# First 64 positions of a retention layer: loads of eight positions a partition, 64x64 score quadrants, keys turned back with the decay

## The chip, the core and the metric

The kernel runs on one core of a Trainium2 chip. The metric is the device time of one execution in microseconds; the number given for a kernel is the median of several executions. TensorE (PE) does the matrix products and writes to PSUM; VectorE (DVE), ScalarE (ACT) and GpSimd (POOL) do the elementwise work; SyncE (SP) only issues transfers. ACT and POOL issue transfers as well, POOL also those that change the type from float32 to float16 on the way.

## What is computed

A retention layer (attention without softmax, with a decay by distance), then a two-layer network with a hard-swish between its layers. Eight batches, eight heads, 576 positions, 64 columns a head; 4608 tokens of 512 columns, 2048 hidden columns.

```python
def _attn_ref(q, k, v):                       # q, k, v: (8, 8, 576, 64)
    scores = D_ ** -0.5 * np.matmul(q, k.transpose(0, 1, 3, 2))
    gamma = 1.0 - 2.0 ** (-5.0 - np.arange(H))
    rel = pos[:, None] - pos[None, :]
    Dmat = np.where(rel >= 0, gamma[:, None, None] ** rel[None, :, :], 0.0)
    return np.matmul(scores * Dmat[None, :, :, :], v)

def _moe_ref(x, w_in, w_out):                 # x: (4608, 512), heads side by side
    h = x @ w_in
    g = h * np.clip(h + 3.0, 0.0, 6.0) / 6.0
    return g @ w_out
```

## The kernel before

**Blocks.** The 576 positions of a batch are cut into the first 64 (`TL`) and four chunks of 128. Block 0 of the network holds the first 64 positions of all eight batches (512 tokens); blocks 1 to 8 hold the 512 other positions of a batch each. Retention runs chunk by chunk with a state of 64x64 a head that is carried along (`zh` from the first 64 positions, then `z`). The network multiplies a block by `w_in` in 16 units (`up_steps`, `ph` products, four steps of 128 rows of `w_in` each), applies the hard-swish on ACT and DVE (L535, L537) and multiplies by `w_out` (`down_plain`, `pd` products; from block 2 on in a seven-product scheme, `pm`).

**Order.** The order of every engine's instructions is the order of the program text; nothing is rearranged. An engine that waits holds up all that stands behind it in its queue. From L771 to L831 the text is the work on the first positions, and the change lies in it, in the functions that it calls, and in `head_states`.

**First positions, loads (L407).** Head pair i holds heads 2i and 2i+1. `load_half` brings one head of q or k of all batches: partition r*8 + b holds positions 4r to 4r+3 of batch b, a row of 256 numbers (1 KB). The source pattern is `r b (j d)` with r of 16. Keys of pair 0 are issued on SP and ACT, queries of pair 0 and 1 on both, queries of pairs 2 and 3 on SP behind the landing of the first half of the keys (`keys`), keys of pairs 1 to 3 on POOL in float16 (2 and 3 behind `keys`). Then POOL issues all values in one transfer (`load_values`, `raw_v`), the first quarter of `w_in` in two halves (rows 0 to 255, then 256 to 511 of `w_in`, L683), and a further quarter. What POOL computes stands behind these issues.

**First positions, work.** `cast_heads` (DVE) turns float32 into float16. `turn_heads` (L440) is eight products against the permuted identity `by_chunk`; each gives one transposed piece of 64x128, columns in the order chunk, batch half, r; ACT copies them out of PSUM (`hqT`, `hkT`). A chunk c of this order is two batches, 128 tokens. `scores_heads` (L471) multiplies 128 keys by 128 queries of a chunk, both batches at once, so half of each result belongs to two different batches. The mask `hmask` (128 columns a head, by ACT from the distances in `dist`) carries the decay and is zero there and above the diagonal; DVE multiplies (`ha`). `values_heads` brings the values into the order of the keys by 16 products of 128x32 a pair (`by_key`), ACT copies. `inner_heads` (L485) multiplies values by masked scores, and one copy a pair puts the result into `xT0`, the input of the network. A few products without use (`idle_products`) stand between.

**First positions, states.** POOL multiplies the float16 keys by a decay for each position (`others`, L138). `keys_heads` (L466) brings a pair into the order of the keys by 16 products, and ACT writes it twice with a factor of 0 or 1 for each partition (`only`), so that `kn[0]` holds the first batch of a chunk and `kn[1]` the second, with zeros elsewhere. `head_states` (L290) makes both states from them. These run at L844, between `pd` products of block 0: `k0 D4 k1 D4 +1 k2 D4 +1 k3 D6 h0 D2 ...` stands for keys of pair 0, four steps of `down_plain`, and so on; `+1` is a pending DVE subtraction on the weights (L552), `h` a call of `head_states`.

Of the kernel before, what the change touches and what calls it, by code (L numbers as in the profile page):

```python
# [21 lines left out]
def kernel(  # L22
# [9 lines left out]
    nc = tc.nc  # L32
# [34 lines left out]
    RP = TL // NJ  # L67
    ii = const.tile([P, NJ + 1], I32)
    ij = const.tile([P, NJ + 6], I32)
    fj = const.tile([P, NJ + 6], FP32)  # L70
    key, odd = fj[:, NJ + 3:NJ + 4], fj[:, NJ + 5:NJ + 6]
    arg = const.tile([P, NJ + 3, 2 * H], FP32)
    dec = const.tile([P, NJ + 3, 2 * H], FP32)
# [5 lines left out]
    query = const.tile([P, P], FP32)  # L79
    early = io.tile([P, H, D], FP32, tag="fv", name="early").rearrange("p h d -> p (h d)")  # L80
    dist, far = early[:, 0:P], early[:, P:2 * P]
    scale = const.tile([P, 1], FP32)
    FAR = 1.0e6
    by_chunk = const.tile([P, P], FP16)
    only = const.tile([P, 2], FP32)
    last = const.tile([P, 1], FP32)
# [3 lines left out]
    def indices():  # L90
        nc.vector.memset(half, 0.5)
        nc.gpsimd.iota(ii[:, 0:NJ], pattern=[[0, NJ]], base=0, channel_multiplier=1)
        nc.gpsimd.iota(ii[:, NJ:NJ + 1], pattern=[[1, 1]], base=0, channel_multiplier=1)
        nc.gpsimd.iota(query, pattern=[[TL, 2], [1, NJ], [NJ, RP]], base=0, channel_multiplier=0,
                       allow_small_or_imprecise_dtypes=True)
        make_identity(nc, ident16)
        p_ = ii[:, NJ:NJ + 1]
        nc.vector.tensor_scalar(ij[:, 0:NJ], ii[:, 0:NJ], P - B, 1, ALU.bitwise_and, ALU.logical_shift_right)
        nc.vector.tensor_copy(ij[:, NJ:NJ + 1], p_)
        for e in range(2):  # L100
            nc.vector.tensor_scalar(ij[:, NJ + 1 + e:NJ + 2 + e], p_, SUB - 1, 1, ALU.bitwise_and,
                                    ALU.logical_shift_left)
        nc.vector.tensor_scalar(ij[:, NJ + 3:NJ + 4], p_, RP - 1, 2, ALU.bitwise_and, ALU.logical_shift_left)
        nc.vector.tensor_scalar(ij[:, NJ + 4:NJ + 5], p_, 5, None, ALU.logical_shift_right)
        nc.vector.tensor_scalar(ij[:, NJ + 5:NJ + 6], p_, 4, 1, ALU.logical_shift_right, ALU.bitwise_and)
        nc.vector.tensor_copy(fj, ij)
        nc.vector.tensor_tensor(fj[:, 0:NJ], fj[:, 0:NJ], query[:, 0:TL:RP], ALU.add)
        nc.vector.tensor_scalar(fj[:, NJ:NJ + 2], fj[:, NJ:NJ + 2], 1.0, -float(P // 2), ALU.mult, ALU.add)
        nc.vector.tensor_scalar(fj[:, NJ + 2:NJ + 3], fj[:, NJ + 2:NJ + 3], 1.0, 1.0 - float(P // 2), ALU.mult, ALU.add)
        nc.vector.tensor_copy(by_chunk.rearrange("p (c e r) -> p c e r", c=NCB, e=2),  # L110
                              ident16.rearrange("p (r e c) -> p c e r", e=2, c=NCB))

    def distances():
        nc.vector.memset(scale, float(np.log(D ** -0.5)))
        nc.vector.tensor_tensor(key, key, fj[:, NJ + 4:NJ + 5], ALU.add)
        nc.vector.scalar_tensor_tensor(out=key, in0=odd, scalar=float(TL), in1=key, op0=ALU.mult, op1=ALU.add)
        nc.vector.tensor_scalar(last, odd, float(TL), float(TL) - 0.5, ALU.mult, ALU.add)
        nc.vector.tensor_scalar(dist, query, key, FAR, ALU.is_lt, ALU.mult)
# [4 lines left out]
    def mask_of_heads(i):  # L123

        for h in (2 * i, 2 * i + 1):
            nc.scalar.activation(hmask[:, h, :], dist, ACTF.Exp, bias=scale, scale=float(np.log(gamma[h])))
# [791 lines left out]
```

## Time and profile before

| | us |
|---|---|
| median of 3 runs | 299.28 (299.08 to 300.13) |
| the profiled execution | 299.44 |
| its span, first to last instruction | 297.7 |
| mean granted TensorE clock, share of full speed | 0.994 |

The page of a profile gives each engine's busy time, the span in 40 slices, the DMA queues with packets and bytes, the chain of work that ended last (followed back from the last instruction to what released each step), and the costliest groups of instructions by line and shape. Further views give the instructions in order of time, the transfers with the time from issue to landing, and the busy time in chosen stretches. `L168` is line 168 of the kernel; the product helper is there, so groups are told apart by names such as `ph` or `pd`. PEld is the loading of weights into TensorE. Landing times of the first transfers, from the DMA view (issue and time to landing):

| transfer | issued on | issue | to landing |
|---|---|---|---|
| hk, pair 0, first and second half | SP, ACT | 0.82, 0.82 | 3.1, 2.6 |
| hk, pairs 1 to 3, six halves | POOL | 1.84 to 5.7 | median 4.8 |
| hq, eight halves | SP, ACT | 1.51 to 5.8 | 4.3 to 5.2 |
| raw_v, 512 KB in float16 | POOL | 6.17 | 7.9 |
| win, first half | POOL | 7.04 | 8.3 |
| win, last piece | POOL | 9.9 | 15.2 |
| wout, last piece | POOL | 15.60 | 19.8 |

Of the engines in the first 20 us, by stretches of 4 us:

| stretch | PE busy | DVE | ACT | POOL | clock |
|---|---|---|---|---|---|
| 0 to 4 | 2.05 | 2.72 | 1.49 | 2.39 | 1.00 |
| 4 to 8 | 2.71 | 1.86 | 2.67 | 3.84 | 1.00 |
| 8 to 12 | 3.52 | 2.67 | 3.58 | 3.81 | 1.00 |
| 12 to 16 | 1.86 | 2.95 | 1.92 | 0.93 | 0.97 |
| 16 to 20 | 4.00 | 0.94 | 1.79 | 3.49 | 0.60 |

### The profile page before, as it was taken

How to read it: one execution, taken by the hardware profiler on the slowest of the kernel's cores; microseconds unless marked ns; L12 is line 12 of the kernel's file. 1: busy time of each engine (PE TensorE's matmuls, PEld its weight loads, DVE VectorE, ACT ScalarE, POOL GpSimd, SP SyncE). 2: the span in 40 equal slices, each digit the busy share in tenths (PEclk: the TensorE clock that was granted, in tenths of full speed). 3: DMA queues.
4: the chain of work that ended last, by engine and by line, in shares of the span. 5: the costliest groups of instructions: out<-in, count | busy, mean ns of one | idle time of the engine just before them, and what ended most of it. 6: DMA issues, size and time to landing. Idle time of an engine off the chain costs nothing.

```text
span 297.7 us, 12581 instructions
## 1 busy us (share of the span) xinstructions
PE 286.3 (96%) x5552; PEld 218.8 (73%) x5552; DVE 211.3 (71%) x374; ACT 193.8 (65%) x350; POOL 133.4 (45%) x169
## 2 busy tenths in 40 slices
PE   5699999999999999999999999999999999999995
PEld 2467566788556667878988787787787788778894
DVE  5629636669885688798866887787769676647654
ACT  5659875789776687586758577566856665655420
POOL 7665078417851912539614862386256013100510
PEclk9979999999999999999999999999999999999999
DMA  7999998989999999998999999789907101200114
GB/s 163 188 205 216 217 233 206 213 184 221 135 214 221 203 205 196 167 234 191 228 244 194 184 216 174 144 168 263 144 27 118 74 2 39 104 5 2 73 73 141
DMA packets 119430, 47.86 MB, mean 161 GB/s; under 512 B 92240, under 2 KB 114768, under 8 KB 119376
## 3 DMA queue, kind: packets, MB, share of 16 engines
q1 hardware_dynamic: 114336, 41.56, 70.6%
q0 software_dynamic: 4608, 5.11, 10.4%
q8 instruction: 43, 0.70, 1.0%
q10 hardware_dynamic: 432, 0.39, 0.5%
q14 instruction: 11, 0.09, 0.2%
HBM read 36.70 MB, written 9.44 MB: 155 GB/s over the span
## 4 chain that ended last, share of the span: by engine, by line
PE 87%; DVE 4%; DMA 4%; ACT 3%; issue 1%; POOL 1%; ACTq 0%
PE ph L168 41%; PE pm L168 29%; PE pd L168 7%; PE po L250 4%; DMA raw_v<-in_v_dram 3%; PE pa L250 2%; DVE ws L552 2%; PE pu L250 1%; DMA hk<-in_k_dram 1%; ACT u L515 1%; DVE g L516 1%; DVE a L285 1%; POOL hk L416 1%; PE hpo L491 1%; PE hpv L459 1%
## 5 line engine op out<-in xcount | busy, mean ns | idle before, releaser
L168 PE MATMUL ph<-xT,win 128*64 128x512 f16 (+1 forms) x1248 | 144.9, 365 | 0.5 <-DVE g L516 0.3
L537 DVE SCALAR_TENSOR_TENSOR g<-u,ph 128x512 f16<-128x512 f32 x132 | 89.2, 683 | 48.5 <-ACT u L535 47.7
L535 ACT ACTIVATE u<-ph,half 128x512 f32<-128x512 f32 x132 | 90.2, 693 | 43.1 <-PE ph L168 40.6
L168 PEld LDWEIGHTS <-win 128*64 128x64 f16 x1248 | 84.5, 136 | 26.5 <-issue 1.9
L168 PEld LDWEIGHTS <-g 128*64 128x64 f16 x928 | 51.0, 110 | 15.6 <-issue 1.1
L168 PEld LDWEIGHTS <-s 128*64 128x64 f16 x896 | 49.9, 110 | 8.4 <-issue 0.5
L334 POOL TENSOR_TENSOR z<-z,gpow 128x256 f32<-128x256 f32 x24 | 16.4, 685 | 75.3 <-DVE z L333 46.9
L168 PE MATMUL pm<-ws,s 128*64 128x256 f16 x672 | 45.6, 273 | 0.1
L386 ACT CAST xT<-po 128x256 f16<-128x256 f32 (+1 forms) x44 | 22.5, 584 | 23.4 <-PE po L250 23.4
L211 POOL TENSOR_TENSOR q<-fq,dec 128x512 f16<-128x512 f32 x32 | 36.7, 1169 | 0.0
L214 POOL TENSOR_TENSOR v<-fv,dec 128x512 f16<-128x512 f32 x32 | 35.5, 1113 | 1.9 <-DMA fv<-in_v_dram 1.9
L168 PE MATMUL pd<-wout,g 128*64 128x512 f16 x256 | 35.0, 382 | 0.2 <-ACT o L581 0.2
L616 POOL TENSOR_TENSOR u<-u,p 128x512 f32<-128x512 f32 x7 | 8.9, 1271 | 54.0 <-ACT u L656 47.8
L168 PE MATMUL pm<-wout,g 128*64 128x256 f16 x448 | 31.6, 273 | 0.4 <-issue 0.4
L285 DVE TENSOR_TENSOR a<-pa,mask 128x256 f16<-128x256 f32 (+1 forms) x44 | 21.9, 539 | 7.8 <-PE pa L250 7.4
L203 ACT CAST k<-fk 128x512 f16<-128x512 f32 x32 | 19.8, 620 | 0.0
L552 DVE TENSOR_TENSOR s<-g 128x1024 f16<-128x1024 f16 x28 | 19.6, 702 | 0.2
L340 ACT CAST z<-z 128x512 f16<-128x512 f32 x24 | 15.0, 625 | 4.2 <-DVE z L330 3.9
L168 PE MATMUL pm<-ws,g 128*64 128x256 f16 x224 | 16.3, 273 | 0.0
L168 PE MATMUL pm<-wout,s 128*64 128x256 f16 x224 | 16.0, 273 | 0.1
L250 PE MATMUL po<-qT,z 64*64 64x64 f16 x512 | 12.6, 198 | 0.7 <-issue 0.4
L552 DVE TENSOR_TENSOR s<-g,s 128x1024 f16<-128x1024 f16 x14 | 12.6, 903 | 0.0
(112 smaller groups left out, 277.7 us busy)
## 6 DMA issues: line engine op xcount, KB each, us to landing
fq<-in_q_dram SPq DMA_DIRECT2D x16, 512.0 KB, 5.9
fk<-in_k_dram SPq DMA_DIRECT2D x32, 256.0 KB, 4.6
fv<-in_v_dram SPq DMA_DIRECT2D x32, 256.0 KB, 5.7
out_dram<-o SPq DMA_DIRECT2D x14, 512.0 KB, 3.2
wout<-in_moe_w_out_dram POOLq DMA_DIRECT2D x4, 512.0 KB, 18.5
out_dram<-o SPq DMA_DIRECT2D x7, 256.0 KB, 3.9
win<-in_moe_w_in_dram POOLq DMA_DIRECT2D x3, 512.0 KB, 13.4
hq<-in_q_dram SPq DMA_DIRECT2D x6, 128.0 KB, 5.0
```

What stands on the lines that cost most here:

```text
L168: nc.tensor.matmul(out[r], lhs[:, r], rhs, skip_group_check=True, **flags)
L203: keys = lambda: nc.scalar.copy(by_head(k16), in_rows(st[c]["fk"]))
L211: nc.gpsimd.tensor_tensor(by_head(q16[:, e]), in_rows(st[c]["fq"][:, :, e, :]), in_rows(dd[:, NJ + 1 + e, 0:H, :]), ALU.mult)
L214: nc.gpsimd.tensor_tensor(v16, st[c]["fv"], dd[:, NJ, H:2 * H, :], ALU.mult)
L250: return lambda: nc.tensor.matmul(*args, skip_group_check=True, **flags)
L285: nc.vector.tensor_tensor(a16[:, a, 0:n].rearrange("p x i q -> p (x i) q"), pa[a].rearrange("p x i q -> p (x i) q"), m, ALU.mult)
L334: nc.gpsimd.tensor_tensor(new, new, decay, ALU.mult)
L340: nc.scalar.copy(z16, zs[c])
L386: nc.scalar.copy(xt[:, s], po[s].rearrange("p x n (e r) -> p x n e r", e=2))
L535: nc.scalar.activation(uu, ph, ACTF.Relu, bias=half, scale=1.0 / 6.0)
L537: nc.vector.scalar_tensor_tensor(out=g[:, hf, :, jr, :], in0=by_half(uu), scalar=1.0, in1=by_half(ph), op0=ALU.min, op1=ALU.mult)
L552: nc.vector.tensor_tensor(*pend.popleft())
```

## The change

Pairs are now heads i and i+4, and group g holds pairs 2g and 2g+1. A transfer brings a whole pair: partition r*16 + (batch, head of the pair) holds positions 8r to 8r+7, a row of 512 numbers (2 KB); r counts 8. The keys are ordered by batch halves: partitions 0 to 63 take batch c, 64 to 127 batch c+4, so that chunk c is batches c and c+4. `turn_heads` has 16 products of 64 columns. The scores are 64x64 quadrants, a batch each, with masks of 64 columns; four products of DVE over two pairs replace eight. `values_heads` has 32 products for two neighbouring heads, against a selection (`selv`) that has zeros for the other half of the positions. `inner_heads` handles a group; ACT and DVE copy one half each. The keys for the states are the turned keys, turned back by eight products and multiplied by the decay on DVE; the copies on ACT, the factors `only` and POOL's products with the decay are gone, and the states read one half of the partitions each. The halves of the first quarter of `w_in` are now rows 0-127 and 256-383, then the others, and block units take the steps in the order 0, 2, 1, 3.

```diff
-    def load_half(i, nm, e, queue, behind=None):
...
-        d = queue.dma_start(hd[i][nm][:, e].rearrange("p j d -> p (j d)"),
-                            dict(q=q, k=k, v=v)[nm][:, 2 * i + e, 0:TL, :].rearrange("b (r j) d -> r b (j d)", j=NJ))
+    def load_heads(i, nm, queue, behind=None):
...
+        d = queue.dma_start(t, dict(q=q, k=k)[nm][:, i::NP, 0:TL, :].rearrange("b e (r j) d -> r (b e) (j d)", j=JL))
...
     def turn_heads(i, nm, copy):
...
-                nc.tensor.matmul(pt[e * D:e * D + D, j, :], hd[i][nm][:, e, j, :], by_chunk, start=True, stop=True,
+                nc.tensor.matmul(pt[e * D:e * D + D, at, :], hd[i][nm][:, j * D:j * D + D], sel[:, e], start=True, stop=True,
...
+    def values_heads(cc, copy):
+
+        pv = psum.tile([P, NCB, 2, D], FP32, tag="pp", name=f"hpv{cc}")
         for c in range(NCB):
+            for x in range(2):
+                for b2 in range(2):
+                    for jp in range(2):
+                        o = slice(SUB * b2 + SUB // 2 * jp, SUB * b2 + SUB // 2 * jp + SUB // 2)
+                        nc.tensor.matmul(pv[o, c], selv[:, x, NCB * b2 + c].rearrange("p y j r -> p (y j r)"),
+                                         raw_v[0][:, 2 * cc:2 * cc + 2, 2 * jp + x, :],
+                                         start=(c == 0 and x == 0), stop=(x == 1), skip_group_check=True)
+        copy(vh[:, :, cc], pv)
...
     def keys_heads(i):
-        pk = by_key(i, "k").rearrange("p c e d -> p c (e d)")
-        for e in range(2):
-            nc.scalar.mul(kn[e][:, i], pk, only[:, e:e + 1])
+        kT = hd[i]["kT"]
+        pk = psum.tile([P, NCB, 2, D], FP32, tag="pp", name=f"hpk{i}")
+        for c in range(NCB):
+            for b2 in range(2):
+                nc.tensor.matmul(pk[rows(b2), c], kT[:, NCB * b2 + c, :], ident16.rearrange("p (e d) -> p e d", e=2),
+                                 start=True, stop=True, skip_group_check=True)
+        dd = dec[:, 0, H + i::NP].unsqueeze(1).unsqueeze(3).to_broadcast([P, NCB, 2, D])
+        nc.vector.tensor_tensor(kn[:, i].rearrange("p c (e d) -> p c e d", e=2), pk, dd, ALU.mult)
+
+    def scores_heads(g):
+        a16 = work.tile([P, 2, 2, NCB, TL], FP16, tag="a16", bufs=4, name=f"ha16_{g}")
+        pa = [psum.tile([P, 2, NCB, TL], FP32, tag="pp", name=f"hpa{e}_{g}") for e in range(2)]
+        for x in range(2):
+            kT, qT = hd[2 * g + x]["kT"], hd[2 * g + x]["qT"]
+            for c in range(NCB):
+                for b2 in range(2):
+                    for e in range(2):
+                        b = NCB * b2 + c
+                        nc.tensor.matmul(pa[e][rows(b2), x, c, :], kT[rows(e), b, :], qT[rows(e), b, :],
+                                         start=True, stop=True, skip_group_check=True)
         for e in range(2):
+            m = hmask[:, NP * e + 2 * g:NP * e + 2 * g + 2, :].unsqueeze(2).to_broadcast([P, 2, NCB, TL])
+            nc.vector.tensor_tensor(a16[:, e], pa[e], m, ALU.mult)
...
+    def inner_heads(g):
...
+        po = [psum.tile([P, 2, NCB, TL], FP32, tag="pp", name=f"hpo{b2}_{g}") for b2 in range(2)]
+        for e in range(2):
+            for c in range(NCB):
+                for x in range(2):
+                    for b2 in range(2):
+                        nc.tensor.matmul(po[b2][rows(x), e, c, :], vh[rows(b2), c, 2 * e + g, x, :], a16[rows(b2), e, x, c, :],
+                                         start=True, stop=True, skip_group_check=True)
+        xt = xts[0][:, g::2, :].rearrange("p e (c b q) -> p b e c q", c=NCB, b=2)
+        nc.scalar.copy(xt[:, 0], po[0])
+        nc.vector.tensor_copy(xt[:, 1], po[1])
```

In `head_states` the left factor becomes `kn[rows(e), i, c, a * D:a * D + D]` and the right one `vh[rows(e), c, j, h2, :]`, with a PSUM bank for each of the two states. The order of the text:

```diff
-        for nm in ("k", "q"):
-            landed = load_half(0, nm, 0, sp)
-            keys = landed if nm == "k" else keys
-            load_half(0, nm, 1, act)
+        keys = load_heads(0, "k", sp)
+        load_heads(0, "q", act)
         nc.scalar.activation(warm, half, ACTF.Exp)
-        load_half(1, "q", 0, sp)
-        load_half(1, "q", 1, act)
+        load_heads(1, "q", sp)
         for i in (2, 3):
-            for e in range(2):
-                load_half(i, "q", e, sp, keys)
+            load_heads(i, "q", sp, keys)
         for i in (1, 2, 3):
-            for e in range(2):
-                load_half(i, "k", e, pool, None if i == 1 else keys)
+            load_heads(i, "k", pool, None if i == 1 else keys)
         load_values()
...
         idle_products(5)
-        mask_of_heads(0)
+        masks_of(0)
         cast_heads(0, "k", on_dve)
         turn_heads(0, "k", on_act)
-        mask_of_heads(1)
-        idle_products(4)
         cast_heads(0, "q", on_dve)
-        mask_of_heads(2)
+        idle_products(2)
         turn_heads(0, "q", on_act)
+        masks_of(1)
+        cast_heads(1, "q", on_dve)
+        idle_products(2)
         turn_heads(1, "k", on_act)
-        cast_heads(1, "q", on_dve)
-        turn_heads(1, "q", on_act)
+        turn_heads(1, "q", on_dve)
         cast_heads(2, "q", on_dve)
+        idle_products(1)
         scores_heads(0)
...
+        turn_heads(3, "q", on_dve)
+        idle_products(1)
+        scores_heads(1)
+        values_heads(0, on_act)
+        values_heads(2, on_dve)
+        values_heads(1, on_act)
+        inner_heads(0)
+        values_heads(3, on_dve)
+        idle_products(3, 1)
         first = [up_steps(0, u) for u in range(4)]
         for dmc in range(3):
             for unit in first:
                 next(unit)
-            if dmc == 1:
-                inner_heads(3, on_act)
+            if dmc == 0:
+                inner_heads(1)
```

## The prediction

> **What bounds the kernel now.** I read the page's totals first, then the chain of work that ended last, then the first 40 us of the timeline, the DMA view there and the stretches of 1 us with their clocks.
>
> ```profile
> span 297.7 us, 12581 instructions
> PE 286.3 (96%) x5552; PEld 218.8 (73%) x5552; DVE 211.3 (71%) x374; ACT 193.8 (65%) x350; POOL 133.4 (45%) x169
> ```
>
> TensorE (PE) is busy 96% of the span: from about 18 us on, where the first `ph` products run, the kernel is a stream of products, and whatever moves the start of that stream moves the end. What sets its start is in the chain:
>
> ```profile
> 0.82 3.06 DMA hk<-in_k_dram
> ...
> 4.16 2.00 POOL hk L416 x4
> 6.17 7.92 DMA raw_v<-in_v_dram
> ...
> 14.12 0.41 PE hpv L459 x16
> ...
> 18.23 2.27 PE ph L168 x8
> 20.50 0.22 PE hpo L491 x4
> 20.72 12.13 PE ph L168 x110
> ```
>
> Columns are start, length, what. The first keys must land (3.88), POOL then issues its remaining key loads and `raw_v` (the values), and everything waits until `raw_v` lands at 14.08. Behind it lie 6.64 us of short work until the 16 early `ph` products and the last `hpo` are through (20.72). The change sits in these two parts and in one short stage at 33 to 41 us.
>
> **The landing of raw_v.** DMA is the limit there: it is busy all the time from 2.3 us, where the first bytes move, 1.5 us behind the issue at 0.82. The ACT queue carries three `hk`/`hq` transfers and nothing else in the whole run:
>
> ```profile
> q10 hardware_dynamic: 432, 0.39, 0.5%
> ```
>
> 432 packets are 144 a transfer: 128 rows of 1 KB and 16 more, one from each engine that took part, as I read it. So before `raw_v` is through, 16 transfers of q and k (2304 packets) and `raw_v` (128 x 8 rows and 16, 1040) pass 16 engines: 209 an engine in 14.08 - 2.3 = 11.8 us, 56 ns each. For rows of 2 KB the five `win` loads give a price: they finish at 25.1 us (issue at 9.9, 15.2 to land), so 2048 rows and 80 closers take 11.0 us behind `raw_v`: 133 an engine, 83 ns each.
>
> After the change, q and k are 8 transfers of 128 rows of 2 KB. Spread over 16 engines, one is 8 x 83 + 56 = 0.72 us an engine, all eight 5.8 us, `raw_v` 65 x 56 = 3.64 us: 2.3 + 9.4 = 11.7 us. A gap comes on top: the four transfers that wait for nothing are through at 2.3 + 4 x 0.72 = 5.2; `hk0` lands at about 4.4, and what waits for it (q2, q3 on SP, k2, k3, `raw_v` on POOL) moves bytes only some 2 us later (0.28 until POOL goes on, 0.2 to issue, 1.5 to the first bytes), at 6.4: 1.2 us. So 12.9, or 1.2 us earlier than now.
>
> But the address pattern changes too. Now its outermost count is 16 (`r`), and 16 engines post a closer; after, `r` counts 8. The trace holds no transfer whose count is below 16, so I bound it. If the eight runs go to eight engines, one transfer is 16 x 83 + 56 = 1.38 us on each of these: `hk0`, `hq0` to `hq3` are 6.9 us there, one or two of the three POOL key loads 1.4 to 2.8 (they may use the other eight), `raw_v` on all sixteen 3.64: 11.9 to 13.3 us from 2.3, and 0.5 us to land: 14.7 to 16.1, or 0.6 to 2.0 later than now. Ends: -1.2 and +2.0. The one row that shows how a transfer is dealt has as many closers as the pattern's outermost count, so I take eight engines and the middle, **+1.3 us**.
>
> [...]
>
> What else lies before `raw_v` stays hidden. With eight engines q3 lands near 12.5 (5 x 1.38 of SP's and ACT's loads, the wait for `hk0`, and the sharing with POOL's); cast 0.48, turn 0.25, copy 0.69, scores 0.45 end at 14.4, a us before 15.4. The masks shrink from 128 to 64 columns, the score products on DVE from eight to four (0.67 each), POOL issues three loads fewer (0.55 each), SP three and ACT two: all under the same wait. If that cover were gone (`raw_v` at 12.9, q3 at 9.2), there would still be over 1 us.
>
> **From raw_v to the stream, now 6.64 us.** PE ran part of it at half clock:
>
> ```profile
> 12.00:13.00 1.00, 0.00 (x0) 0.02 (x1) 1.00 (x3) 0.58 (x1) 0.00 (x0) 1.00 1.23 167
> ...
> 16.00:17.00 1.00, 1.00 (x26) 0.69 (x24) 0.25 (x1) 1.00 (x3) 0.75 (x4) 0.50 1.25 205
> 17.00:18.00 1.00, 1.00 (x26) 0.94 (x20) 0.26 (x1) 0.79 (x2) 0.93 (x6) 0.50 1.24 207
> ```
>
> The last three columns are granted clock, DMA share and GB/s. PE idles 2.1 us ahead of 14.12, and from 15.8 to 19.1 the clock is 0.50. At full clock the 16 early `ph` products (0.108 each, as 110 in 12.13 us) would take 1.73 instead of 2.5, and the `hpv`, `hpo` and `idle` pieces some 0.8 less: 5.1 us in all.
>
> After the change, counted from the landing at full clock. A call of `values_heads` has 32 products instead of 16, at 13.7 ns (16 in 0.22) 0.44 us, and the first product after another shape costs about 0.12 (`hpv` takes 0.34 in the chain where 16 need 0.22). First call done at 0.60; ACT's copy starts 0.08 later (14.12 to 14.58 for 16 products now) and takes 0.60. The second call ends at 1.04, its copy is on DVE (0.69, as the `hpo` copy there): 1.16 to 1.85. `inner_heads(0)` needs both; its second half runs at 1.9, its results are ready near 2.4, and its two copies go side by side on ACT (0.59) and DVE (0.69): 3.1. `ph` starts at 3.15; 16 of them are 1.73, the `inner_heads(1)` between them 0.45 (32 of 64x64 as `pa` at 45.0) and two changes of shape 0.24: 5.57. Against 6.64 that is -1.07, if PE is at full clock. At half clock over the same stretch it loses what it loses now, 1.5: +0.4. Two us of idle PE came before the half clock now, and with q3 at 12.5 the gap would be about 1 us, but with little work in the 5 us before; I take **-0.5**, between the ends. One more cover: `win` half 0 is needed at 18.6 and lands 1.3 behind `raw_v`, at 16.7.
>
> [...]
>
> **Keys and states, 33 to 41 us.**
>
> ```profile
> 32.85 0.34 PE hpk L459 x16
> 33.19 0.98 PE pd L168 x8
> ...
> 38.57 0.25 PE pu L296 x16
> 38.82 0.43 PE pd L168 x4
> ```
>
> `hpk` is 16 products of 128x32 between products of 128x64, and costs 0.34 where its work is 0.22; `pd` behind it 0.98 where eight need 0.86. The new eight products have the shape of `pd`: 4 x 0.23 saved, -0.9. The state products become 64x64 quadrants between `pd` of 128x64; `pa`, of that shape, shows 0.45 for 32 and 1.20 for the ten `pd` behind it, where 1.08 are needed: 4 x 0.2 lost, +0.8. Together -0.1. ACT loses eight `ws<-hpk` (0.687 each, 5.5 us), DVE gets four of about 0.67 and loses none there: the last `g` ends at 34.3, four key copies and two `ws` (0.69) then fill DVE until about 38.3, and `h0` starts at 38.4 now. Its own wait is this:
>
> ```profile
> 35.48 0.69 DVE L552 TENSOR_TENSOR ws<-wout 128x1024 f16<-128x1024 f16 x1 [0.59 <-DMA wout<-in_moe_w_out_dram]
> ```
>
> The last `wout` piece lands at 35.4 and would land at about 36.7; behind that DVE instruction is queued the key copy of pair 3, and PE's `h0` waits for it. PE comes there 0.8 later too, so 0 to 0.4: **+0.1**. POOL is rid of four products with k (1.05 each at 24.6 to 28.7); it idled for 10.3 us after them, so nothing, and the smaller `arg` and `dec` too. ACT's 5.5 us shorten nothing either: PE waits 0.17 us for ACT there in all (before `pd` at 42.77), which bounds that gain.
>
> **Sum.** +1.3 - 0.5 - 0.1 + 0.1 = +0.8 us. The profiled execution took 299.44 us (span 297.7 and 1.74 around it), 0.16 over the median of 299.28. So 300.24 for an execution like it, 300.1 against the median. A run of this kernel tells apart about 0.5%, 1.5 us: this is no measurable change.
>
> **Rivals.**
> *A, the forecast (chance 0.40):* fewer engines for the loads, later values, a shorter tail. Own range 299.0 to 301.2.
>
> *B, the loads keep sixteen engines (0.27):* `raw_v` at 12.9, -1.2 - 0.5 = -1.7: 297.6; with a warm tail 297.0. For it: 2 KB rows move 83 ns against 2 x 56, and fewer issues and closers. Against it: the outermost count of 8.
>
> *C, PE stays at half clock through the tail (0.28):* slower. Place: from the first products to about 21 us. The first `idle` products run at half clock now (0.23 us each, 0.11 later), and the clock rises near 5.3, after 3 us of nearly unbroken work. After, `hk0` lands at about 6 on eight engines, so PE is idle from 4.3 to 6.9, and `idle_products` before the first scores are 10 instead of 9, but spread out. If the rise fails, or falls back for want of work, the tail runs at half: `ph` starts at about 4.5 behind `raw_v` instead of 3.15 and 16 of them end near 7.1 instead of 5.57: +0.5 against now; with `raw_v` at its later end, +2.0, it is +2.5, 301.6. It decides from a gap of about 2 us ahead of `raw_v`, as now. Against it: now the clock held through 6.2 to 7.3 with PE idle.
>
> *D, the changed parts are off the path (0.05):* landing as now, tail as now: 299.3.
>
> **Chances.** Faster by over 0.5% (below 297.8): B's 0.23, A's 0.03: 0.26. Slower (above 300.8): C's 0.26, A's 0.10: 0.36. Within: 0.38. The range takes in B's 297.0 and C's 301.6 with a `raw_v` somewhat beyond the bound (5 x 16 rows on a loaded engine, each 10 ns dearer, are 0.8 us): 296.8 to 302.4.
>
> **What would show it.** `hk`/`hq` transfers of 136 packets (sixteen engines: 144); `hk0` landing at about 6, `raw_v` at 14.7 to 16.1 (B: 12.9); `ph` 3.15 us behind it; the clock column of the tail (C: 0.50 from `raw_v` on); `hpk` at 0.22 and `pu` with wider neighbours at 33 to 42 us. The forecast is wrong if `raw_v` lands before 13.5 or PE's stream from there to the end, 277 us now, changes by over a microsecond.

## The result

The changed kernel takes 307.87 us (median of 6 runs, 306.87 to 308.31), the kernel before beside it 299.18: a ratio of 1.0287 (95% interval 1.0264 to 1.0309). It is 8.7 us slower, where 300.1 was forecast and 302.4 was the end of the range. The profiled execution took 307.79 us against 299.44 before. Traces are of one execution each, so times inside a run are those of that execution.

The totals of the changed kernel's page:

```profile
span 306.1 us, 12856 instructions
...
PE 289.7 (95%) x5710; PEld 223.5 (73%) x5710; DVE 213.9 (70%) x374; ACT 186.6 (61%) x337; POOL 127.8 (42%) x162
```

The span is 8.4 us longer, but PE is busy only 3.4 us more. PE's program has 158 more products and as many more weight loads: 316 instructions. That number turns out to matter most.

The chain of waits of the changed kernel (start, length, what), from the first load to the end of block 0's projection:

```profile
0.82 5.68 DMA hk<-in_k_dram
6.50 0.30 issue
6.81 1.19 POOL hk L402 x2
8.00 10.36 DMA raw_v<-in_v_dram
18.36 0.04 issue
18.40 2.75 PE hpv L449 x72
21.15 0.57 PE hpo L489 x21
21.72 0.22 PE hpv L449 x7
21.94 1.90 issue
23.84 0.55 PE hpv L449 x25
...
26.49 14.08 PE ph L155 x120
```

`hk0` lands at 6.50 (3.88 before) and `raw_v` at 18.36 (14.08). Then comes a step that the chain of before did not have: 1.90 us of "issue" on PE, in the middle of the last `hpv` call. The profile shows no semaphore that PE waits for there: the values have landed, and the 7 products ahead of the pause are of the same call. Last, the `ph` products end at 40.57 (32.85 before).

The 8.4 us by stretches, each from the two chains:

| stretch | before | after | more |
|---|---|---|---|
| to the landing of `raw_v` | 14.08 | 18.36 | 4.28 |
| from there to the end of block 0's `ph` | 18.77 | 22.21 | 3.44 |
| from there to the first `pu` (38.57, 45.65) | 5.72 | 5.08 | -0.64 |
| from there to the `pd` x8 (51.32, 58.77) | 12.75 | 13.12 | 0.37 |
| the rest of the span | 246.38 | 247.33 | 0.95 |

The queues of the changed kernel's page (packets, MB, share of 16 engines), then its DMA view from 6 to 8 us (two lines) and from 9 to 10 us (two lines):

```profile
q8 instruction: 44, 0.72, 1.0%
q10 hardware_dynamic: 136, 0.26, 0.3%
```

```profile
q1 hardware_dynamic: 103, 0.20, 29.4%
q0 software_dynamic: 89, 0.09, 26.7%
...
q0 software_dynamic: 89, 0.09, 57.3%
q1 hardware_dynamic: 66, 0.14, 56.7%
```

The one transfer on q10 (ACT's queue) has 136 packets: 128 rows and 8 more, so eight engines took part, as the prediction reads such a count. The DMA share from 2 to 8 us is about half of what it was: 0.40, 0.52 and 0.56 in stretches of 2 us, where the kernel before had 0.76, 1.09 and 1.21.

No view names the engines of a transfer, but the rates say where POOL's three key loads (queue q0) lay. From 4 to 6 us the loads of SP and ACT alone move 98 rows a us. From 6 to 8 us POOL's first key load moves beside them, and all together make 96 a us, so it shares their eight engines. From 9 to 10 us the second key load and the queries together make 155: the second lies on the other eight. The third, issued within 1.2 us of the second, lands at 15.8 us where the second landed at 12.0, so it is taken to lie on the loaded eight again. On POOL's queue the number of packets does not fall: q0 has 4560 on the page of the changed kernel and 4176 on that of e1 (below), 128 more for each key load.

The clock around the landing and behind it, in stretches of 3 us (the last three columns are granted clock, DMA share and GB/s; the share adds up the time of all packets, so it passes 1 where packets overlap):

```profile
15.00:18.00 3.00, 2.13 (x66) 1.61 (x66) 0.88 (x2) 0.59 (x1) 0.55 (x1) 0.50 1.38 197
18.00:21.00 3.00, 2.74 (x107) 2.58 (x98) 1.94 (x3) 0.59 (x1) 1.95 (x7) 0.50 1.24 206
21.00:24.00 3.00, 1.10 (x59) 0.79 (x55) 0.73 (x2) 1.16 (x2) 2.64 (x16) 0.90 1.24 207
24.00:27.00 3.00, 3.00 (x75) 1.70 (x68) 1.12 (x2) 0.47 (x1) 0.37 (x8) 0.67 1.21 211
27.00:30.00 3.00, 3.00 (x24) 1.54 (x22) 0.26 (x1) 0.54 (x2) 0.00 (x0) 0.76 1.08 216
```

PE waited 2.89 us for keys ahead of 15.86; the clock is at 0.50 from 14.8 to 21.6. The halt of 1.90 us is followed by a second stretch at half clock, from 25.0 to 28.5, in the `ph` products. Before, 15.8 to 19.2 was at half. The column says 1.00 up to the first change that a trace holds, and there the products' own times have to be read: the 16 `hptk` at 7.01 took 0.64 us and those at 12.06 took 0.44, so the first rise came only at about 11.4 us here, against 5.6 in the kernel before.

The end of the keys' stage, from the same chain:

```profile
44.40 0.60 DVE ws L551
44.99 0.61 DVE ws L462
45.61 0.04 issue
45.65 0.22 PE pu L283 x4
```

DVE, which now writes the keys (L462, 0.60 each), ends last there and PE's `pu` waits for it, but the stage as a whole is 0.64 us shorter than before.

### The profile page after: what moved, and what is told of

The parts are those of the page before. It is cut to its first block, busy times and chain, and to the rows that moved or that the text cites. A ratio compares the mean times of both kernels' runs of the same rounds, so it can differ in the third digit from the quotient of the medians.

```text
span 306.1 us, 12856 instructions
## 1 busy us (share of the span) xinstructions
PE 289.7 (95%) x5710; PEld 223.5 (73%) x5710; DVE 213.9 (70%) x374; ACT 186.6 (61%) x337; POOL 127.8 (42%) x162
## 3 DMA queue, kind: packets, MB, share of 16 engines
q0 software_dynamic: 4560, 5.11, 10.1%
## 4 chain that ended last, share of the span: by engine, by line
PE 83%; DVE 5%; DMA 5%; ACT 3%; issue 2%; POOL 0%; ACTq 0%
PE ph L155 41%; PE pm L155 28%; PE pd L155 6%; DMA raw_v<-in_v_dram 3%; PE po L237 3%; PE pa L237 2%; DVE ws L551 2%; DMA hk<-in_k_dram 2%; PE hpv L449 1%; PE pu L237 1%; ACT u L514 1%; DVE ws L462 1%; DVE g L515 1%; DVE a L272 1%; PE ptq L155 1%
## 5 line engine op out<-in xcount | busy, mean ns | idle before, releaser
L155 PE MATMUL ph<-xT,win 128*64 128x512 f16 (+1 forms) x1248 | 147.5, 367 | 2.3 <-issue 1.8
L155 PEld LDWEIGHTS <-win 128*64 128x64 f16 x1248 | 86.3, 136 | 28.8 <-issue 4.9
L155 PEld LDWEIGHTS <-g 128*64 128x64 f16 x928 | 52.6, 110 | 13.8 <-issue 0.4
L155 PEld LDWEIGHTS <-s 128*64 128x64 f16 x896 | 51.4, 110 | 7.4 <-issue 0.5
L321 POOL TENSOR_TENSOR z<-z,gpow 128x256 f32<-128x256 f32 x24 | 16.4, 685 | 75.5 <-DVE z L320 47.5
L155 PE MATMUL pm<-ws,s 128*64 128x256 f16 x672 | 46.3, 273 | 0.1
L373 ACT CAST xT<-po 128x256 f16<-128x256 f32 (+1 forms) x44 | 22.5, 584 | 22.6 <-PE po L237 22.6
L155 PE MATMUL pm<-wout,g 128*64 128x256 f16 x448 | 32.5, 273 | 0.0
L155 PE MATMUL pm<-ws,g 128*64 128x256 f16 x224 | 16.6, 273 | 0.0
L155 PE MATMUL pm<-wout,s 128*64 128x256 f16 x224 | 16.4, 273 | 0.1
```

The source lines that it names most:

```text
L155: nc.tensor.matmul(out[r], lhs[:, r], rhs, skip_group_check=True, **flags)
L321: nc.gpsimd.tensor_tensor(new, new, decay, ALU.mult)
L373: nc.scalar.copy(xt[:, s], po[s].rearrange("p x n (e r) -> p x n e r", e=2))
```

## The experiments

Three theories stood against each other. The loads: eight engines bring the values late, and that is the loss. The clock: PE runs cold for want of work ahead of the values. The third, PE's program: PE's own instructions are brought by DMA, and a halt marked "issue" is PE waiting for the next piece of them. Its reading is from the page: q8 carries "instruction" packets, 44 of 0.72 MB in all, 16.4 KB each. PE's 2 x 5710 products and weight loads make 44.6 groups of 256 (before: 43 packets, 43.4 groups), so I read a packet as a block of 256 instructions of PE, 64 bytes each. Counted from the start of PE's program, the halt of the changed kernel stands where instruction 704 is due, and borders lie at 192, 448, 704 and so on. The number of packets bears this out: 43 borders from 192 on fit into 11,104 instructions (before), 44 into 11,420 (changed), and 45 into 11,464 and 11,488 (e3 and e5 below, whose pages have 45 packets). Ahead of the first `ph` product the kernel before has 434 instructions, the changed one 766.

**e1_sixteen: the changed kernel with loads on sixteen engines.**

```diff
-        ... i::NP, 0:TL, :].rearrange("b e (r j) d -> r (b e) (j d)", j=JL))
+        ... i::NP, 0:TL, :].rearrange("b e (r j) d -> (b e) r (j d)", j=JL))
```

with `sel` permuted to fit.

> The changed kernel with one thing altered: partition (batch, head of the pair)*8 + r instead of r*16 + (batch, head), so the outermost count of the address pattern of the query and key loads is 16 instead of 8 (the selection matrix follows). Theory 1 (the loads are dealt to eight engines, and that moves the landing of the values): 144 packets a transfer again, the first keys land near 4.5 us instead of 6.5, the values near 13 instead of 18.4, and at least the 4.3 us that they came later come back: 303.5 us or less, 298 to 300 if the array's half clock goes with them. Theory 2 (the rearranged work costs it: more and smaller products, their supply with instructions, the clock): the values land early, but the time stays above 304.

306.15 us, 1.0214 (1.0174 to 1.0255). The q10 transfer has 144 packets, `hk0` lands at 5.37 and `raw_v` at 14.65: the loads are cured but for 0.6 us, and only 1.7 us of the 8.7 come back, where the loads alone were expected to give back 4.3. The chain of e1 shows why:

```profile
6.77 7.88 DMA raw_v<-in_v_dram
14.69 0.29 PE hpv L449 x7
14.98 1.39 issue
16.36 2.61 PE hpv L449 x89
18.98 0.40 PE hpo L489 x30
19.38 0.22 PE hpv L449 x7
19.60 2.96 issue
22.56 0.91 PE hpv L449 x25
```

Two halts, 1.39 and 2.96 us. Between them PE executes 89 + 32 + 7 = 128 products (the chain lists 30 of the 32 `hpo`, which overlap the `hpv`), that is 256 instructions. Values that come sooner only meet the late block sooner.

**e2_before_eight: the kernel before with its loads on eight engines.** The pattern is turned from 16 outer runs to 8, and the permutations with it:

```diff
-    ... 0:TL, :].rearrange("b (r j) d -> r b (j d)", j=NJ))
+    ... 0:TL, :].rearrange("b (r j) d -> b r (j d)", j=NJ))
```

> The kernel before with one thing altered: its query and key loads take batch as the outermost dimension (count 8) instead of r (16); the selection matrices and the positions behind the decays follow, the rest is unchanged. Theory 1: 136 packets a transfer; on the loaded engines 16 transfers of 16 rows at 56 ns and the values, so the values land at 18 to 21 us instead of 14.1, and the time is 304 to 308. Theory 2: the pattern's order is of no account, the values land at 14 and the time is 299 within 1 us.

302.61 us, 1.0101 (1.0073 to 1.0129). The page of e2:

```profile
q10 hardware_dynamic: 408, 0.39, 0.4%
```

and a part of its chain:

```profile
17.85 0.62 PE hpv L462 x16
18.47 0.54 PE hpa L481 x8
...
21.79 0.57 PE hpo L494 x4
...
24.51 0.22 PE hpo L494 x8
```

408 are three times 136. `raw_v` lands at 17.81, 3.73 later and just short of the 18 to 21 expected; `ph` ends at 36.86, 4.0 later; there is no halt of 0.3 us or more on the chain. The time stays below the 304 to 308 expected. So the eight engines cost the kernel before some 3.3 us in all, far from 8.7. Of the POOL loads it shows again that they do not all lie on the loaded eight: from 5.0 to 5.5 us the packets of POOL's queue alone have a share of 0.99.

The clock column of e2 is 1.00 throughout, but the products say that PE ran at half clock until about 22.5 us: 16 `hpv` take 0.55 to 0.62 us (0.34 to 0.41 at full clock before), and the step of eight `hpo` takes 0.57 at 21.79 and 0.22 at 24.51. With the keys later, the rise of the clock failed, which is what rival C of the prediction describes. It cost little here: from the landing to the end of `ph` are 19.05 us, 0.28 more than before.

**e4_keys_sixteen: the changed kernel with keys on sixteen engines and queries on eight.** The key pattern is that of e1, the query pattern that of the changed kernel.

> The changed kernel with the keys alone in the order with an outermost count of 16, the queries still at 8. Theory 1: the loaded eight engines carry 4 x 1.38 us of queries, 4 x 0.72 of keys and 3.64 of values: the values land at 14.5 to 16, between the two, and the time lies between the changed kernel and the one with all loads at sixteen. Theory 2: no difference to the changed kernel.

305.76 us, 1.0203 (1.0147 to 1.026). `raw_v` lands at 17.41, later than the 14.5 to 16 expected and 2.8 us later than in e1, and the time is the same. There is one halt, where instruction 704 is due, 1.41 us (21.11 to 22.52), and `ph` ends at 37.76, sooner than in e1 (39.27), which has a further stretch at half clock. So it is not the landing of the values that sets the end here: instruction 704 comes at 22.52 in e4 and at 22.56 in e1.

**e3_warm: the changed kernel with eleven more idle products ahead of the last keys.**

```diff
-        idle_products(1)
+        idle_products(12)
```

> The changed kernel with 11 more idle products (of 128x512, 2.4 us at full clock) in the gap ahead of the last key pair, where the array waits from 12.9 to 15.9 us. The values land at 18.4 as before. If the half clock from 14.8 to 21.7 and from 25 to 28 comes from that gap, the 96 value products take 1.4 us instead of 2.75 and the time falls by 1 to 3 us, to 305 to 307. If not, it stays at 308. The halt of 1.9 us that the profile puts down to nothing (after row 703 of the array's program) comes at the same row if it is the supply with instructions, which is now 22 products earlier in the work, in the first inner products; if it belongs to the value products of the last pair, it stays there.

311.54 us, 1.041 (1.0356 to 1.0465): worse. PE waited 1.48 us for the values in place of 0.26, and the halt moved: with 44 instructions more ahead of it, it stands in the `hpo` products (21.98 to 23.02), where instruction 704 is now due. That the halt keeps to the count and leaves the call speaks for the third theory. The clock theory's cure worked in part: half clock shrank from 10.2 us in the changed kernel to 3.4 (18.4 to 21.8), and `ph` ends 1.7 us sooner, at 38.86. The time rises all the same. In the profiled run (308.80, the lowest of four) the rest of the span is longer, with halts of 0.75, 0.91 and 0.98 at 141.7, 163.6 and 199.7, where the changed kernel has one of 0.91; the other runs, at 311.20 to 312.97, leave no trace, and the rest of the 3.7 us over the changed kernel stays open.

**e6_before_warm and e8_before_ungated: the kernel before with a warm PE.** e6 adds nine idle products ahead of the values; e8 also lets the later loads go without waiting for the first keys.

```diff
+        idle_products(9)
         values_heads(0)
```

> The kernel before with nine more idle products of 512 columns (1.95 us) where the array waits for the values, from 12.0 to 14.1 us. The values land at 14.1 as before. If the half clock from 15.8 to 19.1 comes from that wait, it goes, and with it 1 to 1.5 us: 297.7 to 298.3. If the clock falls for another reason, or its price lies under other waits: 299 within 0.5 us.

> The kernel before with the nine idle products and with no load held back until the first keys have landed. The values land at 13.3 to 14; 297 to 298.3 if the clock holds; no better than the kernel with the idle products alone if the first keys come later in exchange.

e6 takes 301.84 us, 1.0075 (1.0041 to 1.0109), e8 299.38, 1.0018 (0.9989 to 1.0048). Both miss the 297 to 298.3 that a held clock was expected to give. In both profiled runs the half clock of 15.8 to 19.2 is gone, and `ph` ends at 32.53 and 32.70 in place of 32.85. In e6 the first `hpv` product starts 0.18 later and a new halt of 0.49 us stands at instruction 448; without these it would have gained 1.0. So the half clock of the kernel before is worth some 0.3 to 1.0 us to the stream, less than the 1.5 by which the forecast had priced it. Both kernels have a halt of 1.04 to 1.06 us at 138 to 139 us, again at a border (instruction 5312, which is 192 + 20 x 256): the added instructions moved it there. The warm-up brings no gain in the whole; e6's profiled run (299.88) lies near the low end of its ten, and what makes the others up to 3.5 us longer was not traced.

**e5_before_split: the kernel before with its products cut in two.** Turns, scores, values and inner products get two products of 64 columns for each of 128, with the same columns in all and the loads untouched; 802 instructions stand ahead of the first `ph` product.

```diff
-                nc.tensor.matmul(po[h2 * D:h2 * D + D, c, :], vh[:, c, i, h2, :], hd[i]["a16"][:, h2, c, :], ...
+                for z in range(2):
+                    nc.tensor.matmul(po[h2 * D:h2 * D + D, c, D * z:D * z + D], vh[:, c, i, h2, :],
+                                     hd[i]["a16"][:, h2, c, D * z:D * z + D], ...
```

> The kernel before with the products of its first positions cut in two along the moving columns: turns, scores, values and inner products of 128 columns become two of 64. The same columns, copies, loads and data, but 802 rows of the array's program ahead of the first product with the input weights instead of 434 (the changed kernel has 766). Theory 3 (the array's program comes in blocks of 256 rows, borders at rows 191, 447 and 703; a block arrives some 5 to 6.5 us after the one before it was entered): halts at row 447 (in the first value products) and row 703 (in the last), 1 and 2 to 4 us, and 301.5 to 304.5 us. Rival: the number of products is of no account where the columns are the same: 299 within 1 us.

307.27 us, 1.0284 (1.0232 to 1.0337): as large a loss as the change has, with none of its loads, and more than the 301.5 to 304.5 expected. The chain of e5:

```profile
17.88 0.27 PE hpv L461 x9
18.15 2.78 issue
20.93 0.52 PE hpv L461 x23
...
22.56 3.41 PE ph L168 x16
```

A halt of 2.78 us stands where instruction 704 is due; the one expected at 448 did not come. The clock is at half from 16.6 to 26.8, so 16 `ph` products take 3.41 us. `raw_v` lands at 15.09, 1.0 later than before, and `ph` ends at 38.75, 5.9 later. The rest of the loss lies behind it: halts of 0.54, 1.03, 0.69 and 0.99 us at 131, 142, 164 and 199 us, all at borders of 256 instructions, since the border now falls at other places of the work. More instructions for the same columns are enough. The products' own time does not explain it: the timeline shows 32 split `hpv` of 64 columns in 0.43 us at full clock, 16 whole ones in 0.41 before.

**e7_sixteen_ungated: e1 with its loads not held behind the first keys.**

> The changed kernel with loads over sixteen engines (as in the first run) and with no load held back until the first keys have landed. Theory 1 alone: the values land 1 to 2 us earlier than the 14.7 of the first run, and the time falls as much, to 304.5. Theory 3: the array enters its blocks little earlier, so the halts at rows 447 and 703 grow by what the values come earlier, and the time stays within 1 us of 306.

306.19 us, 1.0245 (1.0217 to 1.0273), as e1 and as the third theory had it. The first `hpv` product starts at 13.4 us, 1.3 sooner than in e1, and the halts are 1.04 (to 14.73) and 3.60 (17.05 to 20.65). Another microsecond in the loads is lost in the halt and in the half clock behind it.

**e10_late_weights: e1 with fewer transfers while the block comes.** The later weights are held on POOL until the first inner result is copied.

```diff
-        win_piece(1)
...
-        inner_heads(0)
+        done = inner_heads(0)
+        after(win_piece(1), done)
```

> The kernel e1 with the second and later pieces of the projection weights issued only once the first inner result is copied, so that fewer transfers are under way while PE's rows 448 to 703 run. If a block of 256 rows of PE's program is late because it shares the DMA engines with the loads, the block from row 704 arrives at 18.5 to 20 us in place of 22.56, the halt of 2.96 us shrinks under 1 us and the time falls to 303 to 304 us, unless the weights themselves come late. If the halt does not depend on what else the DMA engines carry, it stays near 3 us and the time at 306.

305.08 us, 1.0188 (1.0145 to 1.0232). PE's timeline in e10 (start, length, what, idle before it), and two of its stretches:

```profile
14.21 0.29 PE L449 MATMUL hpv<-raw_v,selv 128*32 128x128 f16 x7 [0.43 <-DMA raw_v<-in_v_dram]
16.35 2.61 PE L449 MATMUL hpv<-raw_v,selv 128*32 128x128 f16 x89 [1.85 <-issue]
18.89 0.63 PE L489 MATMUL hpo<-ha,ws 64*64 64x64 f16 x32
19.45 0.29 PE L449 MATMUL hpv<-raw_v,selv 128*32 128x128 f16 x7
20.08 0.55 PE L449 MATMUL hpv<-raw_v,selv 128*32 128x128 f16 x25 [0.33 <-issue]
```

```profile
17.00:18.00 1.00, 1.00 (x48) 1.00 (x43) 0.00 (x0) 0.59 (x1) 0.00 (x0) 0.50 0.08 18
18.00:19.00 1.00, 1.00 (x45) 0.80 (x37) 0.69 (x1) 0.00 (x1) 0.00 (x0) 0.50 0.00 0
```

With the loads out of the way (DMA share 0.08 and 0.00, where e1 has 1.24) the second halt falls from 2.96 to 0.33 us, with the same program and the same order on PE. The first, at a moment when the loads of both kernels are alike, stays (1.85). This is the decisive run: the halt depends on what else the DMA engines carry.

The packets of q8 in the DMA view show where the time goes. PE enters the block at instruction 448 at 16.36 us in e1 and at 16.35 in e10. The next packet of q8 starts at 20.20 in e1 and at 17.39 in e10, and lasts about 1 us in both; instruction 704 follows at 22.56 and 20.08. So from the packet's start to the first instruction it is 2.4 and 2.7 us, much alike, and the loads cost the time ahead of the packet: 3.8 us against 1.0. In no run does the packet of a block start earlier than 1.8 us before PE enters the block ahead of it (1.6 in the kernel before, 1.5 in the changed one), so PE has, as I read it, one block in reserve at most. The time gained is small because the weights are now late: `wout` lands at 41.68, and DVE and PE wait for it.

**e11_weights_sooner and e12_weights_at_values: the same, released sooner.** e11 releases the weights behind the copy of the first values, e12 behind their landing. The edit of e11 against e10:

```diff
-        values_heads(0, on_act)
+        done = values_heads(0, on_act)
+        after(win_piece(1), done)
...
-        after(win_piece(1), done)
```

> The kernel e10 with the same weights released some 2.4 us sooner: behind the copy of the first group of values (about 18.0 us) in place of the first inner result (20.4). If in e10 the cured halt was paid for with weights that came late (wout landed 41.68 us), wout now lands at about 39.3, the projection and the keys after it no longer wait there and the time falls by some 2 us to 302 to 303. If the block of PE's program from row 704 is still in the way of the released weights at 18 to 20 us, a part of the halt (up to 2 us) comes back and the time stays at 304 to 305.

> The kernel e11 with the same weights released as soon as the values have landed (some 15 us) in place of the copy of their first group (16.6). The gap in the loads shrinks by about 1.6 us. If two blocks of PE's program need no more of the DMA engines than the 1 to 2 us in which they are then still empty, no halt over 1 us comes back, wout lands at about 36.5 (38.08 in e11), the keys' stage waits for it no longer and the time falls to 300 to 302: beside before within 1%. If the block from row 704 is caught by the released weights, a halt of 1 to 3 us stands at that row again and the time is 303 to 305.

e11 takes 303.31 us, 1.0145 (1.0095 to 1.0194), e12 303.55, 1.0137 (1.0092 to 1.0183). PE's timeline in e11:

```profile
15.08 2.59 PE L449 MATMUL hpv<-raw_v,selv 128*32 128x128 f16 x96 [1.41 <-DMA raw_v<-in_v_dram]
17.60 0.64 PE L489 MATMUL hpo<-ha,ws 64*64 64x64 f16 x32
18.18 1.18 PE L449 MATMUL hpv<-raw_v,selv 128*32 128x128 f16 x32
```

No halt is listed any more; the last 32 `hpv` take 1.18 us, some 0.3 more than a third of the 96 before them, and that is what is left at instruction 704. `raw_v` lands at 15.04 and `ph` ends at 33.86: 18.82 us behind it, where the kernel before has 18.77. Without the halt the changed stretch costs what the old one did. What remains in this profiled run (span 300.2, 2.5 over the kernel before) is the landing, 0.96 later, which is still there when `pu` starts behind `wout` at 39.52 (38.57 before), and 1.55 behind that, with a halt of 0.68 us at 194.2. That run is the lowest of the four; the others took 303.05 to 304.42 and leave no trace.

In e12 the released weights catch the block again, as the second half of its expectation said (part of its chain):

```profile
17.35 0.22 PE hpv L450 x7
17.57 1.41 issue
18.98 0.55 PE hpv L450 x25
```

So within this order there is a trade: what the weights gain in being sooner, the block of PE's program loses. No version here is faster than the kernel before.

**e9_values_first: the kernel before with the values issued ahead of the last two pairs of keys**, and those pairs' turns and inner products moved in among the first steps of the projection.

```diff
         for i in (1, 2, 3):
             ...
-        load_values()
+            if i == 1:
+                values = load_values()
```

> The kernel before with the values issued ahead of the last two pairs of keys, and the last two pairs' turns and inner products moved in among the first steps of the projection. The rows of PE's program stay at some 434 ahead of the first projection product's stream. If the start of the stream is set by the landing of the values (14.08 us before), they land at about 12.2 us, the stream begins at some 16 us in place of 18 and the whole ends 1.5 to 2 us earlier: 297 to 298 us. If the last keys hold the inner products of pairs 2 and 3, with VectorE's mask products of 1.35 us for a pair behind them, the gain is eaten and the time stays at 299.

304.10 us, 1.0158 (1.0118 to 1.0199): a miss. Queries that SP issued at 4.41 landed only at 12.36, PE stood 3.49 us, with the clock at half from 10.1 to 16.9, and stood another 1.70 us for DVE's copy of the last keys, with the clock at half from 20.3 to 23.7. `ph` ends at 37.40. PE's program holds nothing up on its chain. So other waits can fill the same stretch, and the values were not the only thing that the start hung on.

## Why the prediction was wrong

**Fewer engines, +1.3 forecast, 4.28 measured.** The mechanism was right: 136 packets for a load of SP or ACT, `hk0` near 6 (6.50). The size was wrong, beyond the upper end of 2.0 by 2.3 us. It was not the number of loads on the loaded eight: "one or two of the three POOL key loads" held, with two of three as far as the rates tell, and by the prediction's prices that is a landing at 16.1. The step that failed is "11.9 to 13.3 us from 2.3": it lets the loaded engines move rows without a pause from 2.3 us on, and it leaves out for eight engines the gap behind `hk0` that the same paragraph had priced at 1.2 us for sixteen. Seven loads of q and k are 896 rows on these engines, 9.1 us at the 98 rows a us measured from 4 to 6 us. They took about 12, until some 14.3 us. About 0.9 went at the start: 83 rows are through at 4.0 us where that rate from 2.3 on gives 167 (35 GB/s from 2 to 3 us, 174 before). About 1.9 went between 8 us and the end, with the gap behind `hk0` and a slower stretch behind it, whose cause stays open. The values then took 4.1, as priced. The same kind of sum came out too early in e1 (12.9 by the prediction, 14.65 measured) and in e4 (at most 16, 17.41 measured).

**From `raw_v` to the end of the projection's first block, -0.5 forecast, +3.44 measured.** The step that failed is "A call of `values_heads` has 32 products instead of 16, at 13.7 ns (16 in 0.22) 0.44 us". It prices products by duration alone. Twice as many instructions must also be brought, and PE went through those from 448 to 704 in 3.5 us when the next ones took 5.4: the halt of 1.90 us. e5 has as large a loss from more instructions alone, e10 and e11 show that the halt goes when the DMA engines are free, and the packets of q8 show the block coming late. With the halt gone the stretch measured +0.05 (e11), against -0.5.

**Rival C** had the sign, and its mechanism was there: later keys, a late rise of the clock (11.4 us, 5.6 before), and half clock again from 14.8. In e2 the rise failed altogether, as C says, until 22.5 us. C is a smaller part of the loss: in e2 it cost 0.28 us behind the landing, e6 puts the half clock of before at 1.0 us at most, and e11, at half clock from 15.5 to 18.9, needs no longer behind its landing than the kernel before. The half clock in the `ph` products followed the halt of 1.90 us, which C did not have: there 120 of them took 14.08 us, in e11 13.04 (20.82 to 33.86).

**The two losses do not add.** Loads alone +3.3 (e2), instructions alone +8.3 (e5), both +8.7; loads cured -1.7 (e1). The block and the values are waited for at the same time, and the later one counts; e1 and e4, with instruction 704 at the same time behind values 2.8 us apart, show it.

**Keys and states, -0.1 and +0.1 forecast.** -0.64 and +0.37 by the table: together -0.27, as small as forecast. DVE became the last to end there, as the wait for `h0` had been named. `hpk` takes 0.22 (40.38 to 40.60 in the timeline; 0.34 before), and the `pd` x4 behind `pu` 0.55 (0.43 before), as forecast.

**The stream behind it, 0 forecast, +0.95 measured.** From the first long run of `ph` to the end it is 279.6 us (277.0 before), outside the microsecond that the prediction had set as its own limit. Some 1.0 of these 2.6 lie behind 58.77, with a halt of 0.91 us at 199.84. e1, e4, e7, e10 and e12 have such halts of 0.9 to 1.25 us between 195 and 199 us and, some of them, near 230; e11 has 0.68 and 0.48. All of them stand at the same borders, instructions 7872 and 9152 (192 + 30 x 256 and 192 + 35 x 256), among small products that use up instructions fast: in the changed kernel the 256 ahead of 7872 are done in 2.2 us, and the next come 3.1 us after PE entered them. So it is the same supply, and the term was put at nothing because instructions were not counted.

## What to carry to other kernels

Count the instructions as well as the columns: a stage that cuts its products into smaller ones at the same total of columns can be held up by the arrival of the engine's own program (2.78 us in e5), above all where the DMA engines are full of loads (2.96 us in e1, 0.33 in e10 with the loads out of the way). A pause marked "issue" that keeps to steps of 256 instructions, whatever the code there, points to that, as the halts at instructions 448 and 704 did here; test it by holding back the transfers of those microseconds, and expect to trade it against the data held back (`wout` at 41.68 us in e10). An insertion of instructions early in a program also moves every later border, and so can make halts far behind it (1.04 and 1.06 us at 138 to 139 us in e6 and e8). And when a transfer's outermost count falls, as here from 16 to 8 with 136 packets a load in place of 144, price the loads that queue on the remaining engines together, with the gaps between them. Last, where a clock column has shown no change yet, take the clock from the products' own times (here 16 `hptk` in 0.64 us at half clock and in 0.44 at full).

## What the runs showed of the hardware

- PE's program came in blocks of 256 instructions: 44 packets of 16.4 KB on q8 for 44.6 such groups in the changed kernel, and 256 instructions between the two halts of e1. From the first instruction of one block to the first of the next at a halt: 5.4 us in the changed kernel, 6.2 in e1, 5.0 in e4, 5.9 in e7, with the DMA engines full; 3.7 in e10 and in e12, at most 3.1 in e11, with fewer transfers under way, and 2.9 to 3.5 at the halts near 197 us. Of this, 2.7 to 3.8 us lay ahead of the block's packet on q8 with the engines full (3.1 in the changed kernel) and 1.0 to 1.2 in e10, e11 and e12; from the packet's start to the first instruction it was 2.3 to 2.7 (2.3 in the changed kernel). That the next block is asked for only when PE is about to enter the one before it is my reading of these times.
- POOL's key loads of eight outer runs lay in turn on the loaded eight engines, on the other eight and on the loaded eight again, as the rates of the changed kernel tell (96 and 155 rows a us, landings at 12.0 and 15.8).
- Behind the first rise of the clock, a stretch at half clock lasted 3.4 us (before, e3, e10, e11, e12), 6.8 (the changed kernel, e4, e7) or 10.2 (e5).
- Half clock followed single waits of PE of 1.41 us (e11, e12), 1.90 (the changed kernel) and 2.12 (before). It did not follow those of 1.04 (e7), 1.41 (e4) and 1.53 (e10, at 41.59), so the length alone does not decide.
